# A written-out instruction order that counts one SBUF port for VectorE and GpSimd, with work moved between four engines

## The chip, the cores and the metric

The kernel runs on one core of a Trainium2 chip. The metric is the time of one execution in microseconds (us); the median of three runs of the kernel before is 695.69 us (695.14 to 697.32). Five engines work side by side, each through its own queue in order: TensorE (PE in the profile, its weight loads PEld), VectorE (DVE), ScalarE (ACT), GpSimd (POOL) and SyncE (SP, which only issues DMAs here). They meet through semaphores.

## The reference

Banded attention over 2 x 8 heads, 768 positions and 64 columns, then two MLPs on the 1536 tokens x 512 columns that come out:

```python
scores = q @ k.T / 8 - slope[h] * dist       # kept: the last 96 positions and the first 8
a = exp(scores - max); a = a / (sum(a) + 1e-9)
x = (a @ v) laid out as 1536 x 512
x = relu(x @ w_in) ** 2 @ w_out              # 512 -> 2048 -> 512
rms = sqrt(mean(x * x) + 1e-6); xn = x / rms * rms_g
g = xn @ w_gate                              # 512 -> 1536
out = (g * sigmoid(g) * (xn @ w_val)) @ w_out2
```

All inputs are float32 in value; the weights arrive as 64-bit numbers.

## The kernel before

Every large product is made of three matmuls (`mm3`, lines 310 to 323): an operand is split into a high part (a rounded copy, ScalarE, line 306) and a low part (the operand less the high part, line 307, on VectorE or GpSimd as the caller says), and high x high, high x low and low x high are added up in PSUM. A weight block arrives by DMA as 128 x 512 64-bit numbers; `expand` (lines 330 to 356) makes float32 of them with one ScalarE step (345) and four VectorE steps (346, 348, 350, 353), all in SBUF; then `split` makes its two parts. A helper `block` does this for one block, `pair` for two blocks at a time, of which it also forms sums and differences (line 388, GpSimd) for a seven-product scheme (`PRODUCTS`) that the second MLP uses.

Tokens are taken in four chunks of 384 columns. The attention works on 16 slices (4 chunks x 4 pairs of heads) of three tiles of 128 queries each. A slice's keys and queries are split in `prep`: high parts on GpSimd (lines 767 and 775; ScalarE only for the first), low parts on VectorE (769, 777). A tile (`tile`, from line 785) runs: six score matmuls (797); on VectorE a bias with a running minimum (804); on ScalarE the exponential with its sum (808); on GpSimd the addition of 1e-9 (812); on VectorE a reciprocal (815); on GpSimd the scaling of the two heads' probabilities (817); transposes on TensorE (824), an eviction (826) and the product with V (833).

The first MLP's products of chunks 0 to 2 for the first four blocks run beside the attention (`begin`), the rest behind it (`rest`): four groups of four blocks, each over four chunks, each chunk's `first` being 16 groups of three matmuls into a layer with relu and square (`relu2`, lines 413 to 416) and 16 more into the output, added up in y on VectorE (447). In the last group `norm_sum` follows each chunk: squares of y on ScalarE (464), their addition on VectorE (465), a matmul with ones into a PSUM bank (467), a square root (470) and three reciprocals (473). `norm` then forms, for a pair of chunks, the normalized x (494), differences (499, GpSimd) and the parts of all of them (306, 307). The second MLP takes six pairs of blocks, each over two pairs of chunks, through `quad` (lines 519 to 552; additions 535 and 543), the gated product (561, 565) and `final` (output bank added up in y, line 589).

The order of the instructions is written out by a planner (`Plan`, lines 60 to 156). Each operation has an engine, a duration from the formulas of lines 159 to 165, what it reads and writes, and for matmuls a due time, which is handed back to what they need. `solve` goes through planned time and starts, on the engine that is free first, the ready operation with the earliest due time. `emit` then issues all operations by planned start. On the chip the engines keep that order, each in its queue, and go when their semaphores allow. The planner holds the engines to be independent of one another. Ahead of the first real MLP product, spare matmuls (line 1096) fill planned idle time of TensorE.

Of the kernel before, what the change touches and what calls it, by code (L numbers as in the profile page):

```python
# [16 lines left out]
ALU = mybir.AluOpType  # L17
# [27 lines left out]
FILL = 30.0  # L45

# [9 lines left out]
class Op:  # L56
    __slots__ = ("slack", "eng", "dur", "lat", "emit", "deps", "succ", "due", "mode", "start", "end", "left", "ready", "n")


class Plan:  # L60
# [11 lines left out]
    def add(self, eng, dur, emit, r=(), w=(), due=None, mode=None, lat=None, slack=0.0):  # L72
# [4 lines left out]
        o.slack = slack  # L77
        o.deps, o.succ = set(), []
# [15 lines left out]
    def solve(self):  # L94
# [11 lines left out]
        self.fill, done, filling = [], 0, True  # L106
        while done < len(self.ops):
# [14 lines left out]
            o = heappop(ready[e])[2]  # L122
# [19 lines left out]
            free[e] = o.end  # L142
            done += 1
# [17 lines left out]
FAST = lambda n: 0.12 + n / 1920  # L161
ACT = lambda n: 0.10 + n / 1200
POOL1 = lambda n: 0.15 + n / 800
# [36 lines left out]
class Mlp:  # L200
# [101 lines left out]
    def split(self, src, dst, n, rs, ws, eng):  # L302
# [4 lines left out]
        self.op(eng, t(n), lambda: e.tensor_tensor(  # L307
            out=dst()[1], in0=src(), in1=f32(dst()[0]), op=ALU.subtract), rs + [(x, "hi") for x in ws], [(x, "lo") for x in ws])

    def mm3(self, bank, w, a, first, last, width, rs, due=None):  # L310
# [12 lines left out]
        return self.op("PE", dur, go, rs, [("b", bank)], due=due, mode="full")  # L323

# [5 lines left out]
    def expand(self):  # L330
# [16 lines left out]
            out=tl(bits), in0=tl(bits), scalar1=LEAST, scalar2=MOST, op0=ALU.max, op1=ALU.min), rb, rb)  # L347
        self.plan.add("DVE", FAST(512), lambda: v.tensor_scalar(  # L348
            out=bi(), in0=bi(), scalar1=3, scalar2=0x3FFFFFF8, op0=ALU.logical_shift_left, op1=ALU.bitwise_and), rb, rb)
        self.plan.add("DVE", DVE(512), lambda: v.scalar_tensor_tensor(  # L350
            out=bi(), in0=tl(raw)[:, :, 0], scalar=29, in1=bi(), op0=ALU.logical_shift_right, op1=ALU.bitwise_or),
            rr + rb, rb)
        self.plan.add("DVE", DVE(512), lambda: v.scalar_tensor_tensor(  # L353
            out=bi(), in0=tl(raw)[:, :, 1], scalar=-(1 << 30), in1=bi(), op0=ALU.bitwise_and, op1=ALU.bitwise_or),
            rr + rb, rb)
# [12 lines left out]
    def pair(self, key, slots):  # L368
# [6 lines left out]
        def keep(names, slot, parts=2):  # L375
# [6 lines left out]
        self.split(a, sl.get, 512, ra, sl.res, "POOL")  # L382
# [5 lines left out]
        add = lambda o, x, y, op, r, w: self.op("POOL", POOL2(256), lambda: nc.gpsimd.tensor_tensor(  # L388
            out=o(), in0=x(), in1=y(), op=op), r, w)
# [4 lines left out]
        self.split(s, sl2.get, 512, rs, sl2.res, "POOL")  # L394
# [7 lines left out]
        self.split(b, sl4.get, 512, rb, sl4.res, "POOL")  # L402
# [5 lines left out]
    def relu2(self, src, rsrc, act):  # L408
# [8 lines left out]
            out=get()[1], in0=t(), in1=f32(get()[0]), op=ALU.subtract), rt + hi, lo)  # L417
# [35 lines left out]
    def norm_sum(self, c, bank):  # L453
# [3 lines left out]
        for e in range(KD):  # L457
# [7 lines left out]
            self.op("DVE", DVE(CH), lambda t=t: nc.vector.tensor_tensor(out=s(), in0=s(), in1=t(), op=ALU.add), rs + rt, rs)  # L465
# [3 lines left out]
            due=self.clock, mode="full", slack=1.0)  # L469
# [6 lines left out]
    def norm(self, p):  # L476
# [4 lines left out]
        for q in range(2):  # L481
# [10 lines left out]
            def fin(n):  # L492
# [3 lines left out]
                    op0=ALU.mult, op1=ALU.mult), self.yres(e, c) + [("ns", c % 2)], res[n])  # L496

            def diff(n, x, y):
                self.op("POOL", POOL2(CH), lambda: nc.gpsimd.tensor_tensor(
                    out=tmp[n](), in0=tmp[x](), in1=tmp[y](), op=ALU.subtract), res[x] + res[y], res[n])  # L500

            def part(n):
                get, r = where[n]
                self.split(tmp[n], get, CH, res[n], r, "DVE")
# [94 lines left out]
    def weights(self, kind, g):  # L599

        if kind == "in" or kind == "out":
            for f in range(G1):
# [10 lines left out]
                self.block((kind, g * G1 + f), slot, "POOL")  # L613
        elif kind == "out2":
            self.used.setdefault(g, [])
            for f in range(2):
                slot = self.ring.popleft()
                self.used[g].append(slot)
                self.block((kind, 2 * g + f), slot, "POOL")
# [11 lines left out]
    def rest(self, clock):  # L631
# [21 lines left out]
        for kind in ("val", "out2"):  # L653
            self.weights(kind, 0)
        self.norm(1)
# [45 lines left out]
class Attention:  # L701
# [53 lines left out]
    def prep(self, s):  # L755

        nc, tl, i = self.nc, self.tl, s % 2
        for n, part in enumerate(self.pieces(s)):
# [5 lines left out]
            if n == 1:  # L764
                hp = self.slices[s][1]
                inv = lambda: tl("inv")[:, hp : hp + 1]
                self.op("POOL", POOL1(w), lambda raw=raw, hi=hi: nc.gpsimd.tensor_scalar(
                    out=hi(), in0=raw(), scalar1=inv(), scalar2=1.0, op0=ALU.mult, op1=ALU.mult), rr + ["inv"], rh)
# [404 lines left out]
```

## Time and profile before

| | |
|---|---|
| median of three runs | 695.69 us |
| profiled execution, its span | 696.2 us, 694.3 us |
| PE busy, PEld busy | 655.4 us (94%), 589.1 us (85%) |
| DVE busy | 487.7 us (70%) |
| ACT busy | 375.0 us (54%) |
| POOL busy | 262.7 us (38%) |
| mean granted TensorE clock | 0.992 |
| HBM read, written | 48.76 MB, 3.15 MB |

Busy time is from the first to the last cycle of an instruction as the profiler has it. Matmuls overlap, so PE busy overstates what TensorE did. A VectorE instruction that has begun but stands for something counts as busy. The stages by time: attention to about 164 us (with the first MLP's first products from 29 us), the rest of the first MLP to 394 us, the second MLP from about 395 us to 689 us, with the norm's work from 336 to 428 us among both.

### The profile page before, as it was taken

What the parts mean: (1) busy time and instruction counts of PE and PEld (TensorE: products, weight loads), DVE (VectorE), ACT (ScalarE), POOL (GpSimd) and SP (SyncE); (2) the same over time, 40 slices, a digit from 0 to 9 for tenths busy, and PEclk for the clock granted to TensorE, in tenths of its full rate; (3) what the DMA queues carried; (4) which work ended last, traced back from release to release, by engine and by line L of the source; (5) the groups of instructions that cost most, each with busy time, mean ns of one, the idle gap of its engine ahead of it and who ended that gap; (6) DMA issues with size and microseconds to landing.
All of it is one profiled execution on the core that took longest, in us unless ns stands there. A gap on an engine that the chain in (4) does not pass through costs nothing.

```text
span 694.3 us, 10667 instructions
## 1 busy us (share of the span) xinstructions
PE 655.4 (94%) x3827; PEld 589.1 (85%) x3827; DVE 487.7 (70%) x978; ACT 375.0 (54%) x834; POOL 262.7 (38%) x338
## 2 busy tenths in 40 slices
PE   5989999998999999999999888999999999999996
PEld 4667777777998999999999776899898898997994
DVE  6988964553889755238769999785966867768434
ACT  3758777776655554345655776554353443443320
POOL 3887855653333020015205245435144423342000
PEclk9989999999999999999999999999999999999999
DMA  5454443110443303002200000231120311210023
GB/s 197 157 171 155 141 141 91 61 46 3 134 139 121 122 22 102 0 1 92 72 21 1 31 30 25 69 121 31 61 91 31 112 62 41 92 61 0 2 76 110
DMA packets 18159, 52.69 MB, mean 76 GB/s; under 512 B 2608, under 2 KB 3888, under 8 KB 18096
## 3 DMA queue, kind: packets, MB, share of 16 engines
q1 hardware_dynamic: 18096, 51.92, 23.2%
q8 instruction: 32, 0.52, 0.3%
q14 instruction: 31, 0.25, 0.1%
HBM read 48.76 MB, written 3.15 MB: 75 GB/s over the span
## 4 chain that ended last, share of the span: by engine, by line
PE 68%; DVE 22%; ACT 4%; issue 2%; POOL 2%; DMA 0%; DVEq 0%; ACTq 0%; POOLq 0%
PE b L316 20%; PE b L317 19%; PE b L318 19%; PE ps L797 4%; PE av L833 3%; PE tb L824 3%; DVE wbits L350 3%; DVE wbits L348 3%; DVE h L416 2%; DVE wbits L346 2%; DVE wbits L353 2%; DVE xl L307 1%; DVE ra L565 1%; DVE h L307 1%; DVE nq L494 1%
## 5 line engine op out<-in xcount | busy, mean ns | idle before, releaser
L307 POOL TENSOR_TENSOR M<-wbits,M 128x512 fp32r<-128x512 f32 x68 | 94.1, 1385 | 207.9 <-ACT M L306 142.4
L316 PE MATMUL b<-xh,M 128*128 128x384 f32 x336 | 117.3, 349 | 2.5 <-DVE ra L565 1.3
L317 PE MATMUL b<-xl,M 128*128 128x384 f32 x336 | 114.2, 340 | 1.1 <-DVE xl L307 1.1
L318 PE MATMUL b<-xh,M 128*128 128x384 f32 x336 | 113.8, 339 | 0.5 <-POOL M L307 0.5
L316 PEld LDWEIGHTS b<-xh,M 128*128 128x128 f32 x336 | 63.9, 190 | 6.8 <-DVE ra L565 1.6
L416 DVE TENSOR_TENSOR h<-ra,h 128x384 fp32r<-128x384 f32 x64 | 43.7, 688 | 36.0 <-ACT ra L415 36.0
L317 PEld LDWEIGHTS b<-xl,M 128*128 128x128 f32 x336 | 64.0, 190 | 3.7 <-DVE xl L307 2.3
L817 POOL TENSOR_SCALAR p<-p,rs 128x256 f32<-128x256 f32 (+1 forms) x96 | 57.4, 610 | 21.7 <-DVE rs L815 20.3
L318 PEld LDWEIGHTS b<-xh,M 128*128 128x128 f32 x336 | 64.0, 190 | 0.8 <-POOL M L307 0.8
L306 ACT CAST M<-wbits 128x512 fp32r<-128x512 f32 x68 | 41.9, 617 | 40.2 <-DVE wbits L353 15.5
L317 PE MATMUL b<-h,M 128*128 128x384 f32 x176 | 59.8, 340 | 3.3 <-DVE h L416 3.3
L316 PE MATMUL b<-h,M 128*128 128x384 f32 x176 | 61.7, 350 | 0.3 <-ACT h L414 0.3
L589 DVE TENSOR_TENSOR y<-b,y 128x512 f32<-128x512 f32 x60 | 40.9, 688 | 28.5 <-PE b L318 28.1
L808 ACT ACTIVATE p<-p,mn 128x256 f32<-128x256 f32 (+1 forms) x96 | 46.7, 487 | 24.4 <-DVE mn L804 20.2
L316 PE MATMUL b<-M,h 128*128 128x512 f32 x144 | 56.6, 393 | 3.1 <-DVE y L589 3.0
L345 ACT ACTIVATE wbits<-wraw 128x512 f32<-128x512 f32 x68 | 45.2, 666 | 26.1 <-DMA wraw<-in_w_gate_dram 10.9
L318 PE MATMUL b<-h,M 128*128 128x384 f32 x176 | 59.0, 335 | 0.0
L350 DVE SCALAR_TENSOR_TENSOR wbits<-wraw,wbits 128x512 int32<-128x512 int32 x68 | 57.7, 848 | 1.7
L318 PE MATMUL b<-M,h 128*128 128x512 f32 x144 | 56.8, 395 | 0.8 <-DVE h L307 0.8
L317 PE MATMUL b<-M,h 128*128 128x512 f32 x144 | 56.6, 393 | 0.0
L353 DVE SCALAR_TENSOR_TENSOR wbits<-wraw,wbits 128x512 int32<-128x512 int32 x68 | 53.5, 791 | 1.1
L413 ACT ACTIVATE ra<-b 128x384 f32<-128x384 f32 x64 | 31.1, 486 | 38.9 <-PE b L318 37.7
(124 smaller groups left out, 1604.6 us busy)
## 6 DMA issues: line engine op xcount, KB each, us to landing
wraw<-in_w_out_dram SPq DMA_DIRECT2D x28, 512.0 KB, 3.4
wraw<-in_w_in_dram SPq DMA_DIRECT2D x16, 512.0 KB, 3.4
wraw<-in_w_gate_dram SPq DMA_DIRECT2D x12, 512.0 KB, 3.4
wraw<-in_w_val_dram SPq DMA_DIRECT2D x12, 512.0 KB, 3.4
raw<-in_kq_dram SPq DMA_DIRECT2D x8, 480.0 KB, 3.5
v<-in_vab_dram SPq DMA_DIRECT2D x8, 384.0 KB, 3.1
out_dram<-y SPq DMA_DIRECT2D x12, 256.0 KB, 2.3
raw<-in_kq_dram SPq DMA_DIRECT2D x7, 416.0 KB, 3.5
```

What stands on the lines that cost most here:

```text
L306: self.op("ACT", ACT(n), lambda: nc.scalar.copy(dst()[0], src()), rs, [(x, "hi") for x in ws])
L307: self.op(eng, t(n), lambda: e.tensor_tensor(out=dst()[1], in0=src(), in1=f32(dst()[0]), op=ALU.subtract), rs + [(x, "hi") for x in ws], [ ...
L316: nc.tensor.matmul(ps, lhsT=wh, rhs=ah, start=first, stop=False, skip_group_check=True)
L317: nc.tensor.matmul(ps, lhsT=wh, rhs=al, start=False, stop=False, skip_group_check=True)
L318: nc.tensor.matmul(ps, lhsT=wl, rhs=ah, start=False, stop=last, skip_group_check=True)
L345: self.plan.add("ACT", ACT(512), lambda: nc.scalar.activation(tl(bits), f32(tl(raw)[:, :, 1]), AF.Abs), rr, rb)
L350: self.plan.add("DVE", DVE(512), lambda: v.scalar_tensor_tensor(out=bi(), in0=tl(raw)[:, :, 0], scalar=29, in1=bi(), op0=ALU.logical_shift ...
L353: self.plan.add("DVE", DVE(512), lambda: v.scalar_tensor_tensor(out=bi(), in0=tl(raw)[:, :, 1], scalar=-(1 << 30), in1=bi(), op0=ALU.bitwi ...
L416: self.op("DVE", DVE(CH), lambda: nc.vector.tensor_tensor(out=get()[1], in0=t(), in1=f32(get()[0]), op=ALU.subtract), rt + hi, lo)
L589: self.op("DVE", DVE(DM), lambda tok=tok, ps=ps: nc.vector.tensor_tensor(out=self.o(tok), in0=ps(), in1=self.o(tok), op=ALU.add), [("b", b ...
L808: self.op("ACT", 0.33 + w / 1200, lambda j=j: nc.scalar.activation(tl(f"p{m}")[:, j, :w], tl(f"p{m}")[:, j, :w], AF.Exp, bias=tl(f"mn{m}") ...
L817: self.op("POOL", 0.2 + w / 800, lambda j=j: nc.gpsimd.tensor_scalar(out=tl(f"p{m}")[:, j, :w], in0=tl(f"p{m}")[:, j, :w], scalar1=rs()[:, ...
```

## The change

The planner gets a second resource: an operation can be marked as a user of the port that VectorE and GpSimd share. All GpSimd operations are, and VectorE's that read two SBUF operands or are marked so; operations with a PSUM operand are not. A port user starts no earlier than the end of the last port user on either engine; while the port is held, an engine takes a ready operation that doesn't use it, if it has one. Planned durations of four kinds are lowered (`FAST`, `ACT`, `POOL1`, and the costs of 804, 808, 815).

Engines change for four kinds of work: the scaling of probabilities goes from GpSimd to VectorE, the high parts of queries and keys from GpSimd to ScalarE, the low parts of the first eight weight blocks (`LO0`) and the differences of the norm from GpSimd to VectorE. What stays on GpSimd: the addition of 1e-9, all other low parts of weights, and the sums of line 388.

The matmul of the squares' sum of a chunk moves behind the next chunk's `first` and goes to bank 7 (before: bank 0 or 1, behind its own chunk), with a due time 12 us ahead of the planned clock there; the last chunk's stays at its end, in bank 1, behind the first weights of the second MLP. The first pair's norm thus follows chunk 2 and not chunk 1 in the program. The slack before such a matmul falls from 1.0 to 0.5 us.

```diff
+LO0, LO1, LOG, LOS = "DVE", "POOL", "POOL", "POOL"
+DIFF = ("DVE", "DVE")
+PART = ("DVE", "DVE")
+SUMS = "POOL"
+SCALE = ("DVE", "DVE")
+QHI = KHI = "ACT"
+EPS = "POOL"
+NSLACK = 0.5
...
+        o.port = eng == "POOL" if port is None else port
...
-            o = heappop(ready[e])[2]
+            if held > t + 0.05 and any(not x[2].port for x in ready[e]):
+                o = min(x for x in ready[e] if not x[2].port)[2]
+                ready[e].remove((o.due, o.n, o))
+                ready[e].sort()
+            else:
+                o = heappop(ready[e])[2]
+            if o.port:
+                t = max(t, held)
...
+            if o.port:
+                held = o.end
...
-FAST = lambda n: 0.12 + n / 1920
-ACT = lambda n: 0.10 + n / 1200
-POOL1 = lambda n: 0.15 + n / 800
+FAST = lambda n: 0.07 + n / 1920
+ACT = lambda n: 0.07 + n / 1200
+POOL1 = lambda n: 0.08 + n / 960
...
-            due=self.clock, mode="full", slack=1.0)
+            due=self.clock - (12.0 if bank == 7 else 0.0), mode="full", slack=NSLACK)
...
-                self.op("POOL", POOL2(CH), lambda: nc.gpsimd.tensor_tensor(
-                    out=tmp[n](), in0=tmp[x](), in1=tmp[y](), op=ALU.subtract), res[x] + res[y], res[n])
+                self.op(DIFF[p], POOL2(CH) if DIFF[p] == "POOL" else DVE(CH), lambda: self.eng(DIFF[p]).tensor_tensor(
+                    out=tmp[n](), in0=tmp[x](), in1=tmp[y](), op=ALU.subtract), res[x] + res[y], res[n], port=True)
...
-                self.block((kind, g * G1 + f), slot, "POOL")
+                self.block((kind, g * G1 + f), slot, LO0 if g == 0 else LO1)
...
-                if g == N1 - 1:
-                    self.norm_sum(c, c % 2)
-                    if c == 1:
+                if g == N1 - 1 and c:
+                    self.norm_sum(c - 1, 7)
+                    if c == 2:
                         self.norm(0)
...
+        self.norm_sum(NC_ - 1, 1)
         self.norm(1)
...
+                if QHI == "ACT":
+                    self.op("ACT", ACT(w), lambda raw=raw, hi=hi, inv=inv: nc.scalar.activation(
+                        hi(), raw(), AF.Copy, scale=inv()), rr + ["inv"], rh)
...
-            if s == 0:
+            if s == 0 or KHI == "ACT":
                 self.op("ACT", ACT(w), lambda raw=raw, hi=hi: nc.scalar.copy(hi(), raw()), rr, rh)
...
-            self.op("POOL", 0.2 + w / 800, lambda j=j: nc.gpsimd.tensor_scalar(
+            e = SCALE[j]
+            self.op(e, 0.12 + w / 760 if e == "POOL" else FAST(w), lambda j=j, e=e: self.mlp.eng(e).tensor_scalar(
                 out=tl(f"p{m}")[:, j, :w], in0=tl(f"p{m}")[:, j, :w], scalar1=rs()[:, j : j + 1], scalar2=1.0,
-                op0=ALU.mult, op1=ALU.mult), [("rs", m), ("p", m, j)], [("p", m, j)])
+                op0=ALU.mult, op1=ALU.mult), [("rs", m), ("p", m, j)], [("p", m, j)], port=True)
```

## Rows read from the trace of the kernel before

**Rows 1.** Stretches, columns: length, busy us (instructions) of each engine, clock, DMA.

```profile
280.00:300.00 20.00, 20.00 (x117) 20.00 (x116) 6.06 (x11) 6.18 (x12) 0.00 (x0) 1.00 0.00 1
499.00:546.50 47.50, 46.31 (x241) 42.62 (x240) 35.22 (x63) 20.28 (x41) 17.28 (x16) 1.00 0.20 67
```

**Rows 2.** Stretches, the five stages: PE, PEld, DVE, ACT, POOL busy, clock, DMA.

```profile
20.00:80.00 60.00, 54.95 (x412) 40.86 (x409) 52.42 (x144) 43.98 (x127) 50.53 (x76) 0.94 0.51 162
80.00:160.00 80.00, 80.00 (x639) 63.16 (x638) 45.38 (x171) 59.67 (x175) 45.53 (x94) 1.00 0.29 87
160.00:380.00 220.00, 213.51 (x1228) 208.88 (x1228) 146.97 (x232) 122.40 (x236) 54.96 (x46) 1.00 0.21 65
380.00:440.00 60.00, 51.88 (x255) 45.21 (x254) 54.70 (x82) 40.02 (x81) 28.89 (x25) 0.97 0.11 36
440.00:680.00 240.00, 234.49 (x1218) 215.92 (x1217) 168.96 (x292) 100.82 (x198) 73.54 (x68) 1.00 0.18 60
```

**Rows 3.** Waits of TensorE, whole span: us in total, times, longest.

```profile
PE b L317 <- DVE h L416: 5.6, 11, 1.2
...
PE b L316 <- DVE y L589: 3.0, 4, 0.8
```

**Rows 4.** Timeline, 43 to 46 us: start, us, what, idle time before it.

```profile
43.46 1.26 POOL L307 TENSOR_TENSOR M<-wbits,M 128x512 fp32r<-128x512 f32 x1
43.52 1.61 DVE L769 SCALAR_TENSOR_TENSOR kql<-raw,inv,kqh 128x384 fp32r<-128x384 f32 x1 [0.40 <-POOL kqh L767]
...
45.71 0.69 PE L833 MATMUL av<-pt,v 128*64 128x128 f32 x4 [2.14 <-issue]
```

**Rows 5.** Single lines: durations in ns, min/median/max, first and last start.

```profile
L348 DVE TENSOR_SCALAR wbits<-wbits x68: 410/427/1521, 14.0 to 633.3; 128x512 int32<-128x512 int32 x68
L350 DVE SCALAR_TENSOR_TENSOR wbits<-wraw,wbits x68: 680/693/1773, 16.3 to 635.1; 128x512 int32<-128x512 int32 x68
L769 DVE SCALAR_TENSOR_TENSOR kql<-raw,inv,kqh x16: 597/827/1644, 8.0 to 140.6; 128x384 fp32r<-128x384 f32 x16
L817 POOL TENSOR_SCALAR p<-p,rs x96: 368/480/1293, 13.7 to 160.4; 128x256 f32<-128x256 f32 x80, 128x128 f32<-128x128 f32 x16
```

**Rows 6.** Stretches of 5 us, columns as in rows 2.

```profile
45.00:50.00 5.00, 4.29 (x19) 3.33 (x20) 3.99 (x16) 1.98 (x6) 2.92 (x7) 0.53 0.57 172
```

**Rows 7.** Timeline, 539 to 544 us.

```profile
539.99 1.29 POOL L307 TENSOR_TENSOR M<-wbits,M 128x512 fp32r<-128x512 f32 x1 [6.07 <-ACT M L306]
540.11 1.72 DVE L350 SCALAR_TENSOR_TENSOR wbits<-wraw,wbits 128x512 int32<-128x512 int32 x1
...
543.21 0.51 PE L316 MATMUL b<-M,h 128*128 128x512 f32 x1 [0.75 <-DVE y L589]
```

**Rows 8.** Groups by line and form: busy us, mean ns, idle before.

```profile
L499 POOL TENSOR_TENSOR nq<-nq,nq 128x384 f32<-128x384 f32 x16 | 20.2, 1264 | 45.7 <-DVE nq L494 40.2 <-ACT h L306 2.6 <-ACT y L586 2.5
L465 DVE TENSOR_TENSOR ns<-ns,nq 128x384 f32<-128x384 f32 x12 | 8.0, 669 | 0.8 <-ACT nq L464 0.2
L773 ACT CAST kqh<-raw 128x448 fp32r<-128x448 f32 x1 | 0.6, 564 | 2.9 <-DMA raw<-in_kq_dram 2.9
L864 DVE TENSOR_SCALAR rel<-y 128x256 f32<-128x256 f32 x1 | 0.3, 286 | 0.0
```

**Rows 9.** Stretch 20 to 80 us, of lines 348, 353, 769 and 817 alone.

```profile
20.00:80.00 60.00, 5.22 (x8) 0.94 0.51 162
20.00:80.00 60.00, 7.68 (x8) 0.94 0.51 162
20.00:80.00 60.00, 7.13 (x6) 0.94 0.51 162
20.00:80.00 60.00, 24.67 (x38) 0.94 0.51 162
```

**Rows 10.** Timeline about 339 us; line 467 alone, durations as in rows 5.

```profile
338.77 1.02 DVE L447 TENSOR_TENSOR y<-b,y 128x384 f32<-128x384 f32 x2
...
L467 PE MATMUL b<-ns,ones x8: 483/486/590, 342.6 to 399.2; 128*128 128x384 f32 x8
```

More of the change, by code (lines that the diff above doesn't have):

```diff
@@ L56 @@
 class Op:
-    __slots__ = ("slack", "eng", "dur", "lat", "emit", "deps", "succ", "due", "mode", "start", "end", "left", "ready", "n")
+    __slots__ = ("slack", "port", "eng", "dur", "lat", "emit", "deps", "succ", "due", "mode", "start", "end", "left", "ready", "n")
 class Plan:
@@ L70, in __init__, with add @@
         self.last_fill = None
-    def add(self, eng, dur, emit, r=(), w=(), due=None, mode=None, lat=None, slack=0.0):
+    def add(self, eng, dur, emit, r=(), w=(), due=None, mode=None, lat=None, slack=0.0, port=None):
         o = Op()
@@ L105, in solve @@
                 heappush(wait[o.eng], (0.0, o.n, o))
-        self.fill, done, filling = [], 0, True
+        self.fill, done, filling, held = [], 0, True, 0.0
         while done < len(self.ops):
@@ L307, in split @@
         self.op(eng, t(n), lambda: e.tensor_tensor(
-            out=dst()[1], in0=src(), in1=f32(dst()[0]), op=ALU.subtract), rs + [(x, "hi") for x in ws], [(x, "lo") for x in ws])
+            out=dst()[1], in0=src(), in1=f32(dst()[0]), op=ALU.subtract), rs + [(x, "hi") for x in ws], [(x, "lo") for x in ws], port=not psum)
     def mm3(self, bank, w, a, first, last, width, rs, due=None):
@@ L323, in mm3, with eng @@
         return self.op("PE", dur, go, rs, [("b", bank)], due=due, mode="full")
+    def eng(self, name):
+        return self.nc.vector if name == "DVE" else self.nc.gpsimd
     def both(self, res):
@@ L381, in pair @@
         sl = slots()
-        self.split(a, sl.get, 512, ra, sl.res, "POOL")
+        self.split(a, sl.get, 512, ra, sl.res, LOG)
         keep(("A11", "A12"), sl)
@@ L387, in pair @@
         s, rs = (lambda: tl(f"wbits{n}")), [("bits", n)]
-        add = lambda o, x, y, op, r, w: self.op("POOL", POOL2(256), lambda: nc.gpsimd.tensor_tensor(
-            out=o(), in0=x(), in1=y(), op=op), r, w)
+        add = lambda o, x, y, op, r, w: self.op(
+            SUMS, POOL2(256) if SUMS == "POOL" else DVE(256), lambda: self.eng(SUMS).tensor_tensor(
+                out=o(), in0=x(), in1=y(), op=op), r, w, port=True)
         R = lambda x, i: (lambda: row(x)[:, i])
@@ L393, in pair @@
         sl2 = slots()
-        self.split(s, sl2.get, 512, rs, sl2.res, "POOL")
+        self.split(s, sl2.get, 512, rs, sl2.res, LOS)
         keep(("S1", "S2"), sl2)
@@ L401, in pair @@
         sl4 = slots()
-        self.split(b, sl4.get, 512, rb, sl4.res, "POOL")
+        self.split(b, sl4.get, 512, rb, sl4.res, LOS)
         keep(("S3", "S4"), sl4)
@@ L416, in relu2 @@
         self.op("DVE", DVE(CH), lambda: nc.vector.tensor_tensor(
-            out=get()[1], in0=t(), in1=f32(get()[0]), op=ALU.subtract), rt + hi, lo)
+            out=get()[1], in0=t(), in1=f32(get()[0]), op=ALU.subtract), rt + hi, lo, port=True)
     def first(self, g, c, banks, dues=None, k_major=False):
@@ L464, in norm_sum @@
             self.op("ACT", ACT(CH), lambda e=e, t=t: nc.scalar.activation(t(), self.y(e, c), AF.Square), self.yres(e, c), rt)
-            self.op("DVE", DVE(CH), lambda t=t: nc.vector.tensor_tensor(out=s(), in0=s(), in1=t(), op=ALU.add), rs + rt, rs)
+            self.op("DVE", DVE(CH), lambda t=t: nc.vector.tensor_tensor(out=s(), in0=s(), in1=t(), op=ALU.add), rs + rt, rs, port=True)
         ps = lambda: tl(f"b{bank}")[:, :CH]
@@ L618, in weights @@
                 self.used[g].append(slot)
-                self.block((kind, 2 * g + f), slot, "POOL")
+                self.block((kind, 2 * g + f), slot, LOG)
         else:
@@ L777, in prep @@
             self.op("DVE", DVE(w), lambda raw=raw, hi=hi, lo=lo: nc.vector.tensor_tensor(
-                out=lo(), in0=raw(), in1=f32(hi()), op=ALU.subtract), rr + rh, rl)
+                out=lo(), in0=raw(), in1=f32(hi()), op=ALU.subtract), rr + rh, rl, port=True)
     def at(self, n):
@@ L803, in tile @@
             name = "rel" if i else "t0"
-            self.op("DVE", DVE(w) + 0.09, lambda j=j, name=name: nc.vector.tensor_tensor_reduce(
+            self.op("DVE", DVE(w) + 0.01, lambda j=j, name=name: nc.vector.tensor_tensor_reduce(
                 out=tl(f"p{m}")[:, j, :w], in0=tl(f"ps{j}")[:, :w], in1=tl(name)[:, :w], scale=-0.125 * slope8(2 * hp + j), scalar=3.0e38,
@@ L839, in tile @@
             x = lambda: self.mlp.x(hp, c * CH, c * CH + CH)
-            self.mlp.split(lambda: tl("av"), x, CH, [("av", a) for a in range(NT)], self.mlp.xres(hp, c * CH, c * CH + CH), "DVE")
+            self.mlp.split(lambda: tl("av"), x, CH, [("av", a) for a in range(NT)], self.mlp.xres(hp, c * CH, c * CH + CH), "DVE", True)
     def masks(self):
```

27 lines of the change are left out of this document (14 added, 13 removed).

## The prediction

> **What bounds the kernel now.** I read the busy table of the page first, then the stages, then the waits of TensorE, then single stretches of the timeline. TensorE is called busy for 94% of the span, but a busy matmul overlaps its neighbour, so I count matmuls instead. In 280 to 300 us nothing disturbs TensorE: 117 matmuls in 20 us, 0.171 us each [rows 1]. Against that pace each stage shows what it loses [rows 2]:
>
> - 20 to 80 us (attention with the first MLP chunk beside it): 412 matmuls in 60 us, while 80 to 160 us, the same mix, runs 639 in 80 us (0.125 us each). 67 are missing, 8.4 us.
> - 80 to 160 us: TensorE is busy throughout; I count no loss.
> - 160 to 380 us (first MLP): 1228 matmuls x 0.171 = 210 of 220 us; 10 us lost, some of it the last attention tile.
> - 380 to 440 us (norm, and the step to the second MLP): 255 matmuls, 43.6 us at 0.171, about 46 us since the wide ones of the output take longer: 14 us lost.
> - 440 to 680 us (second MLP): one pair of blocks takes 47.5 us and has 240 matmuls [rows 1], 168 of 384 columns and 72 of 512. At 0.171 and 0.228 (0.171 x 512/384, an estimate) that is 45.1 us: 2.4 us lost in each of five, 12 us.
>
> So some 44 us of 696 are TensorE's to win; the head of the span and the tail behind the last matmul stay. The Trainium skill ("Trainium Kernel Development and Optimization", Performance Expectations) calls matmul busy time a bad measure and weight-load busy time a good one. By matmul busy, 440 to 680 us loses 5.5 us, by weight loads 24 us; my count lies between them, and the sum does not use either.
>
> Why TensorE waits: VectorE is late. The waits name line 416 (5.6 us) and line 589 (3.0 us), both VectorE [rows 3]. And VectorE is late where GpSimd runs: at 43.46 us GpSimd starts a lo part of 1.26 us; VectorE's line 769, begun 0.06 us later, takes 1.61 us instead of its 0.60 as if it had begun when GpSimd ended; TensorE then stands 2.14 us [rows 4, 5], and behind that its granted clock is 0.53 in 45 to 50 us [rows 6], nearly all at the lower level (1.2 of 2.4 GHz). Over the whole stage the clock is 0.94, so 0.06 x 60 = 3.6 us of full-speed work are gone; over 380 to 440 us it is 0.97, 1.8 us [rows 2]. In the second MLP a lo part on GpSimd at 539.99 us turns line 350's 0.69 us into 1.72 us, and TensorE waits 0.75 us at 543.21 us for the addition queued behind it [rows 5, 7].
>
> The Trainium skill ("SBUF — State Buffer", SBUF: two separate sides) says that VectorE (two SBUF inputs, or a two-port mode) and GpSimd share a port pair as an exclusive lock for whole instructions. The trace agrees: 1.01 us too long beside a 1.26 us operation.
>
> **The change part by part.**
>
> *The plan treats port users as one resource.* It issues no instruction. It can only order: while a GpSimd operation holds the port, VectorE is given work that reads PSUM. What it is worth is the VectorE lateness that it hides, bounded below by a loss (an order that is worse for TensorE) and above by the losses counted above. In 440 to 680 us no engine assignment of the weights changes, so this part acts alone there; a pair shows a wait of 0.75 us [rows 7], and the pipe runs empty and refills around it, which I put at as much again. I take 1 of the 2.4 us in each of five: **-5 us** (+3 to -10).
>
> *Scaling of probabilities, POOL to VectorE.* 96 instructions leave POOL (480 ns median [rows 5]). On VectorE the nearest row is line 864's 128x256 tensor_scalar, 0.286 us [rows 8]; by half of line 348's 0.427 us for 512 it would be 0.21 us [rows 5], by POOL's own price 0.48 us. I take 0.286, which has the same shape and engine. A GpSimd-to-TensorE hop becomes a VectorE-to-TensorE hop, and two scales shorten by 2 x 0.19 us in a tile's chain.
>
> *Lo parts of the first eight blocks, POOL to VectorE.* 8 x 0.69 us (line 350's clean price, same 512 width and SBUF inputs [rows 5]) = 5.5 us more VectorE.
>
> *High parts of K and Q, POOL to ScalarE.* 31 casts at up to 0.564 us [rows 8], some 17 us on ScalarE over the attention. In 80 to 160 us about half of them fall, 9 us on 59.7 busy of 80 [rows 2]: covered. Without that cover they would cost their 17 us; I cost them nothing.
>
> *What the opening comes to.* VectorE is busy 52.4 of 60 us in 20 to 80 us [rows 2]. Lines 348, 353 and 769 hold 5.22 - 8 x 0.427 = 1.8, 7.68 - 8 x 0.69 = 2.2 (353 by line 350's clean price, the same shape) and 7.13 - 6 x 0.60 = 3.5 us of waiting behind GpSimd [rows 5, 9], 7.5 us, which goes when GpSimd has little left there but the small addition of 1e-9. Added: 38 scales [rows 9] x 0.286 = 10.9, and 5.5. Result 52.4 - 7.5 + 16.4 = 61.3 of 60; with the low price of the scale 58, with POOL's price and no contention gone 76. So the opening stays bound by VectorE, with some of its weight work put off: the 2.14 us stall and the 3.6 us of slow clock can go, but VectorE has no room to give all of it. I take **-2 us** (+8 to -8).
>
> *160 to 380 us.* Lo parts of the later blocks and the sums stay on POOL; only the order is new. Of line 416's waits, 5.6 us in all [rows 3], I put most of it here, since the line runs 64 times and only the first chunks fall into the attention; I read its lateness as line 350's. I take **-4 us** (+2 to -8).
>
> *The norm.* 16 differences go from POOL (1.264 us) to VectorE; the nearest VectorE row is line 465, 0.669 us with waiting in it [rows 8]. 380 to 440 us has nine of them: VectorE gains about 9 x 0.55 = 5 us of work (0.55 is 0.669 less its waiting, an estimate) and is busy 54.7 of 60 already [rows 2], but it loses the waiting behind 11 us of GpSimd. The difference sits between two VectorE steps, so 0.6 to 0.7 us and two hops go from each link of a chain. The sum's matmul moves to bank 7 and behind the next chunk's first layer: for chunks 0 to 2 that is at least 8 us later than the chunk's end (16 groups of 3 x 0.171), where it now comes about 3 us after (chunk 0's last addition ends at 339.8 us, its sum's matmul starts at 342.6 us [rows 10]); the first norm has a whole chunk more to spare, so I cost it nothing; if it hadn't, the price is the 5 us between. What is late next is the second norm, from the last chunk, whose sum keeps bank 1. It stays a VectorE chain. I take **-5 us**, 1.8 of it clock (+4 to -10).
>
> *Slack 0.5 for 1.0 and the new prices:* a planned matmul comes up to 0.5 us earlier, four times: between -2 and +2 us, nothing taken.
>
> Sum: 2 + 4 + 5 + 5 = 16 us. The profiled execution took 696.2 us (span 694.3 and 1.9 around it), so 680.2; the median of the three runs is 0.5 us below the profiled one: **680 us**.
>
> **The rivals.**
>
> 1. *The forecast* (680, own range 672 to 688): half of the second MLP's and a third of the other losses go. For it: the stretched operations stand directly ahead of TensorE's waits. Against: VectorE's load in two stages.
> 2. *The order fills the opening and the norm too.* With chains shortened and the slow-clock stretches gone, 20 to 80 us gives 6 us more, the norm 4, the first MLP 5: 665 us. For it: all four losses have VectorE waiting behind GpSimd. Against: 61.3 of 60 us.
> 3. *The plan's port does not meet the chip's.* Engines run on semaphores, not on planned times; a GpSimd operation half a microsecond off collides with another VectorE operation instead, and the waits move. Then only work leaving POOL counts, and VectorE pays it back: 690 to 700, around 695.
> 4. *VectorE becomes the bound of the opening: slower.* Place: 20 to 80 us and the norm. Price: if scales cost 0.35 us (a quarter over the row, between it and POOL's 0.48) and contention stays, VectorE needs 52.4 + 13.3 + 5.5 = 71.2 us, 11.2 over; with 5 us won back in the two MLPs, 696.2 + 11.2 - 5 = 702 us. It decides once VectorE's work there passes 60 us by more than can be put off to 80 to 160 us, where it is busy 45 of 80: a block's expansion is 2 x 0.43 + 2 x 0.69 = 2.2 us [rows 5], two blocks can wait, so from about 64 us. The lock that the Trainium skill names ("SBUF — State Buffer", the same section) speaks against the change: a two-port scale also shuts out POOL's addition of 1e-9, which stays in the tile's chain; no row here shows that pair. Had each of 48 tiles to wait a scale's 0.286 us, 14 us would come, mostly beside other tiles, and the time would be that of this rival.
>
> **How the numbers follow.** Chances: forecast 0.48, rival 2 0.22, rival 3 0.14, rival 4 0.16. What can be told from no change is 0.3%, 2.1 us. Faster: 0.48 + 0.22 + 0.06 of rival 3 = 0.76; within: 0.07 (rival 3, and a little of 4); slower: 0.17. Range: a tenth lies below 663 (beyond rival 2) and a tenth above 698 (most of rival 4), so 663 to 698.
>
> **What would show it.** Right: lines 348, 350 and 353 with means near 0.43 and 0.69 us; no clock below 0.9 between 40 and 60 us; line 589's waits under 1.5 us; the pair of blocks at 46.5 us instead of 47.5; line 416's waits halved. Wrong: VectorE at 57 or more of 60 us with fewer than 412 matmuls in 20 to 80 us (rival 4), attention's last tile after 162 us, a norm whose matmul of squares is waited for, or the waits of line 416 and 589 as long as now under other names (rival 3).

## The result and the profile after

The changed kernel takes 677.57 us (median of four runs, 676.58 to 680.09) against 695.54 us of the kernel before beside it: a ratio of 0.9742, 95% interval 0.9711 to 0.9774. The profiled execution is the slowest of the four, 680.09 us with a span of 678.3 us, 16.1 us less than the profiled one of before.

The same five stretches as in [rows 2], of the changed kernel:

```profile
20.00:80.00 60.00, 56.89 (x408) 42.58 (x407) 55.40 (x185) 50.17 (x135) 5.42 (x17) 0.89 0.50 157
80.00:160.00 80.00, 79.56 (x625) 61.52 (x626) 58.38 (x226) 64.29 (x188) 6.06 (x27) 1.00 0.28 91
160.00:380.00 220.00, 217.64 (x1254) 215.60 (x1251) 148.29 (x250) 128.97 (x251) 47.88 (x38) 0.99 0.20 65
380.00:440.00 60.00, 54.60 (x271) 49.61 (x270) 52.98 (x92) 37.87 (x73) 17.86 (x16) 0.91 0.11 36
440.00:680.00 240.00, 231.52 (x1204) 214.04 (x1202) 167.19 (x291) 94.82 (x191) 71.53 (x66) 0.99 0.20 67
```

GpSimd is almost gone from the attention (50.5 to 5.4 us in the first stretch), but TensorE has no more matmuls there (408 for 412). The first MLP has 26 more in the same 220 us; the last stretch ends behind the kernel's last matmul now, so its count can't be compared. Pairs of blocks of the second MLP can: each pair but the first makes twelve additions into y (line 611, 589 before). The 49th of them starts here, before and now:

```profile
663.63 0.69 DVE L589 TENSOR_TENSOR y<-b,y 128x512 f32<-128x512 f32 x1 [0.83 <-PE b L318]
```

```profile
647.47 0.69 DVE L611 TENSOR_TENSOR y<-b,y 128x512 f32<-128x512 f32 x1 [0.83 <-PE b L336]
```

The first starts at 474.2 and 464.2 us (further down), so four pairs take 189.4 us before and 183.3 us now, about 47.4 and 45.8 us each. In the stretch of one pair, 45.2 us long now, TensorE doesn't stop (in [rows 1] it was busy for 46.31 of 47.5):

```profile
484.60:529.80 45.20, 45.20 (x239) 42.22 (x238) 34.80 (x62) 19.34 (x40) 16.82 (x16) 1.00 0.22 70
```

TensorE's longest waits are in other places than in [rows 3]. Line 438 is line 416 of before, and line 611, the addition into y of the second MLP, is in no row. The longest is for a high part of the attention's first slice (2.9 us before); the next two rows lie at 401 to 408 us, in the second norm:

```profile
PE ps L824 <- ACT kqh L791: 3.2, 1, 3.2
PE b L334 <- ACT xh L324: 2.8, 2, 1.6
PE b L335 <- DVE xl L325: 2.0, 2, 1.2
...
PE b L335 <- DVE h L438: 0.7, 1, 0.7
```

Where the 16 us come from is read off three lines, by first and last start: the product with V (its last start ends the attention), the addition into y of the first MLP, and that of the second. Of the kernel before:

```profile
L833 PE MATMUL av<-pt,v x352: 272/273/473, 17.7 to 164.1; 128*64 128x128 f32 x176
L447 DVE TENSOR_TENSOR y<-b,y x48: 494/552/558, 197.3 to 394.3; 128x384 f32<-128x384 f32 x48
L589 DVE TENSOR_TENSOR y<-b,y x60: 681/691/693, 474.2 to 688.5; 128x512 f32<-128x512 f32 x60
```

Of the changed one:

```profile
L861 PE MATMUL av<-pt,v x352: 272/273/476, 15.2 to 163.3; 128*64 128x128 f32 x176
L469 DVE TENSOR_TENSOR y<-b,y x48: 494/551/558, 195.7 to 389.4; 128x384 f32<-128x384 f32 x48
L611 DVE TENSOR_TENSOR y<-b,y x60: 674/691/692, 464.2 to 672.3; 128x512 f32<-128x512 f32 x60
```

Attention 164.1 to 163.3 us (-0.8). First MLP, from there to its last addition, 230.2 to 226.1 (-4.1). The norm with the first pair of blocks, to the second MLP's first addition, 79.9 to 74.8 (-5.1). The rest of the second MLP 214.3 to 208.1 (-6.2). The sum is 16.2 us.

The border between the first MLP and the norm is not the same place in the two orders. The two stages before and now (columns as in [rows 2]):

```profile
164.10:394.30 230.20, 223.13 (x1265) 217.89 (x1260) 160.22 (x253) 131.46 (x256) 57.86 (x47) 1.00 0.20 65
394.30:474.20 79.90, 73.14 (x370) 65.91 (x369) 68.94 (x108) 49.51 (x96) 37.17 (x33) 0.98 0.17 53
```

```profile
163.30:389.40 226.10, 224.47 (x1283) 222.99 (x1280) 157.35 (x264) 133.15 (x259) 49.99 (x40) 0.99 0.20 66
389.40:464.20 74.80, 69.40 (x349) 63.44 (x348) 61.36 (x107) 47.70 (x91) 26.18 (x24) 0.93 0.15 50
```

Now 18 matmuls more stand ahead of the border and 21 fewer behind it, 3 to 4 us at the 0.171 us of [rows 1] (an estimate). TensorE's idle time (length less busy) fell from 7.1 to 1.6 us in the first MLP and from 6.8 to 5.4 us in the norm. So only the sum of the two, 9.2 us, can be compared between kernels, and most of it was won in the first MLP.

TensorE's clock did not mend in this execution but fell earlier: it is at its lower level from 25 to 35 us and again in the norm.

```profile
25.00:30.00 5.00, 5.00 (x26) 3.35 (x27) 4.18 (x19) 3.48 (x12) 1.05 (x2) 0.50 0.50 166
30.00:35.00 5.00, 5.00 (x27) 3.21 (x23) 4.40 (x15) 3.78 (x11) 0.26 (x1) 0.50 0.44 157
...
405.00:410.00 5.00, 3.11 (x7) 2.21 (x8) 4.86 (x10) 2.29 (x5) 0.00 (x0) 0.50 0.00 0
```

### The profile page after: what moved, and what is told of

Its sections match the earlier page's. It is cut to its first block, busy times and chain, and to the rows that moved or that the text cites. A ratio compares the mean times of both kernels' runs of the same rounds, so it can differ in the third digit from the quotient of the medians.

```text
span 678.3 us, 10579 instructions
## 1 busy us (share of the span) xinstructions
PE 653.2 (96%) x3823; PEld 592.3 (87%) x3823; DVE 496.6 (73%) x1098; ACT 387.6 (57%) x865; POOL 152.2 (22%) x187
## 5 line engine op out<-in xcount | busy, mean ns | idle before, releaser
L325 POOL TENSOR_TENSOR M<-wbits,M 128x512 fp32r<-128x512 f32 x60 | 83.0, 1387 | 246.3 <-ACT M L324 194.6
L438 DVE TENSOR_TENSOR h<-ra,h 128x384 fp32r<-128x384 f32 x64 | 37.3, 586 | 49.0 <-ACT ra L437 49.0
L435 ACT ACTIVATE ra<-b 128x384 f32<-128x384 f32 x64 | 31.2, 487 | 47.5 <-PE b L336 47.2
L366 ACT ACTIVATE wbits<-wraw 128x512 f32<-128x512 f32 x68 | 45.2, 668 | 20.7 <-DMA wraw<-in_w_in_dram 8.0
L371 DVE SCALAR_TENSOR_TENSOR wbits<-wraw,wbits 128x512 int32<-128x512 int32 x68 | 55.1, 811 | 1.5
L374 DVE SCALAR_TENSOR_TENSOR wbits<-wraw,wbits 128x512 int32<-128x512 int32 x68 | 48.4, 714 | 0.9
L839 POOL TENSOR_SCALAR rs<-sm 128x2 f32<-128x2 f32 x48 | 12.7, 265 | 143.4 <-ACT p L835 143.4
```

Of the source, the lines that this page charges most:

```text
L325: self.op(eng, t(n), lambda: e.tensor_tensor(out=dst()[1], in0=src(), in1=f32(dst()[0]), op=ALU.subtract), rs + [(x, "hi") for x in ws], [ ...
L366: self.plan.add("ACT", ACT(512), lambda: nc.scalar.activation(tl(bits), f32(tl(raw)[:, :, 1]), AF.Abs), rr, rb)
L435: self.op("ACT", ACT(CH), lambda: nc.scalar.activation(t(), src(), AF.Relu), rsrc, rt)
L438: self.op("DVE", DVE(CH), lambda: nc.vector.tensor_tensor(out=get()[1], in0=t(), in1=f32(get()[0]), op=ALU.subtract), rt + hi, lo, port=True)
```

## The experiments

The table has what every run gave, the four stages worked out as above from each kernel's own three lines (times in us, one profile each), and the ratio to the kernel before on the same chip. The first MLP and the norm are to be read together, as said above.

| kernel | attention | first MLP | norm | second MLP | median | ratio, 95% interval |
|---|---|---|---|---|---|---|
| before | 164.1 | 230.2 | 79.9 | 214.3 | 695.5 | 1 |
| changed | 163.3 | 226.1 | 74.8 | 208.1 | 677.57 | 0.9742 (0.9711 to 0.9774) |
| after_again | 164.4 | 224.6 | 75.2 | 208.2 | 677.92 | 0.9734 (0.9718 to 0.9751) |
| fill45 (same instructions) | 161.3 | 226.1 | 75.2 | 208.1 | 678.39 | 0.9747 (0.9724 to 0.9770) |
| plan_only | 163.9 | 226.1 | 74.4 | 208.2 | 680.53 | 0.9780 (0.9747 to 0.9813) |
| no_port | 161.3 | 236.8 | 80.5 | 214.3 | 700.45 | 1.0066 (1.0041 to 1.0091) |
| no_port_old_prices | 163.5 | 232.7 | 79.0 | 214.3 | 696.27 | 1.0025 (0.9995 to 1.0055) |
| no_port_mean | 171.6 | 227.5 | 75.7 | 208.3 | 690.85 | 0.9936 (0.9914 to 0.9957) |
| scale_pool | 159.0 | 226.2 | 73.9 | 208.1 | 675.83 | 0.9709 (0.9692 to 0.9727) |
| low_dve | 160.5 | 225.6 | 75.3 | 207.8 | 677.02 | 0.9728 (0.9706 to 0.9750) |
| norm_old | 162.0 | 222.6 | 77.0 | 208.1 | 675.57 | 0.9712 (0.9687 to 0.9738) |
| old_prices | 158.9 | 225.6 | 76.0 | 208.1 | 676.46 | 0.9729 (0.9711 to 0.9747) |
| norm_warm | 160.5 | 226.1 | 74.7 | 207.2 | 676.09 | 0.9725 (0.9703 to 0.9746) |
| best | 156.9 | 226.2 | 74.7 | 207.1 | 674.89 | 0.9696 (0.9676 to 0.9716) |

**plan_only: the new order and prices, no work moved.**

```diff
-LO0, LO1, LOG, LOS = "DVE", "POOL", "POOL", "POOL"
-DIFF = ("DVE", "DVE")
-SCALE = ("DVE", "DVE")
-QHI = KHI = "ACT"
-NSLACK = 0.5
+LO0, LO1, LOG, LOS = "POOL", "POOL", "POOL", "POOL"
+DIFF = ("POOL", "POOL")
+SCALE = ("POOL", "POOL")
+QHI = KHI = "POOL"
+NSLACK = 1.0
...
-                if g == N1 - 1 and c:
-                    self.norm_sum(c - 1, 7)
-                    if c == 2:
+                if g == N1 - 1:
+                    self.norm_sum(c, c % 2)
+                    if c == 1:
...
-        self.norm_sum(NC_ - 1, 1)
```

> The new planner with the port and the new prices, but every engine as before (scales, high parts of K and Q, low parts of the first eight blocks, differences all on GpSimd) and the squares' sum in its old place. Theory A (the order around the port wins the two MLPs; the moved work wins the norm): first MLP 4 us and second MLP 5 to 6 us shorter as in the changed kernel, pair of blocks near 45.3 us, opening and norm as before or a little better, 683 to 687 us. Rival B (the win is the work that left GpSimd, the plan's port doesn't meet the chip's): MLPs as before with the waits of line 589's kind still there, 692 to 697 us. Rival C (the opening suffers when a busy GpSimd is serialized in the plan): MLPs shorter but attention ends 5 us or more later, 688 to 692 us.

Its three lines:

```profile
L860 PE MATMUL av<-pt,v x352: 272/273/473, 17.4 to 163.9; 128*64 128x128 f32 x176
L469 DVE TENSOR_TENSOR y<-b,y x48: 496/557/559, 194.8 to 390.0; 128x384 f32<-128x384 f32 x48
L611 DVE TENSOR_TENSOR y<-b,y x60: 674/692/693, 464.4 to 672.6; 128x512 f32<-128x512 f32 x60
```

680.53 us: with every engine where it was, the new order wins some 15 of the 18 us, and more than theory A gave it, because the first MLP and the norm together (300.5 us) are as short as in the changed kernel (300.9, before 310.1). Rival B falls.

**no_port: the moved work, ordered without the port.**

```diff
-        o.port = eng == "POOL" if port is None else port
+        o.port = False
```

> The changed kernel with the port mark false for every operation, so the planner again holds VectorE and GpSimd independent; engines, prices and the place of the squares' sum stay as changed. Theory A: the second MLP goes back to 47 us or more per pair of blocks, line 611 (the addition into y) is waited for again, the first MLP gives back about 4 us, the norm keeps most of its gain, the opening is within 2 us of the changed kernel: 686 to 690 us. Rival B: everything stays, 676 to 680 us.

```profile
L861 PE MATMUL av<-pt,v x352: 272/273/476, 15.7 to 161.3; 128*64 128x128 f32 x176
L469 DVE TENSOR_TENSOR y<-b,y x48: 542/557/558, 194.6 to 398.1; 128x384 f32<-128x384 f32 x48
L611 DVE TENSOR_TENSOR y<-b,y x60: 683/691/692, 478.6 to 692.9; 128x512 f32<-128x512 f32 x60
```

700.45 us, worse than theory A's 686 to 690 and 0.7% slower than before. The waits are back under their new line numbers. From 160 to 400 us (first row) and from 440 us on (the two others):

```profile
PE b L335 <- DVE h L438: 8.6, 8, 2.3
```

```profile
PE b L334 <- DVE ra L565: 3.4, 6, 1.0
PE b L334 <- DVE y L611: 3.0, 4, 0.8
```

The second MLP is to the tenth that of before (214.3). The first MLP and the norm together take 317.3 us, 7.2 more than before, and 6.6 of them are in the first MLP, where of the moved work only the squares' sum and the first norm's differences fall. What else is different there are the prices, which the next kernel put back.

**no_port_old_prices.**

```diff
-        o.port = eng == "POOL" if port is None else port
+        o.port = False
...
-FAST = lambda n: 0.07 + n / 1920
-ACT = lambda n: 0.07 + n / 1200
-POOL1 = lambda n: 0.08 + n / 960
+FAST = lambda n: 0.12 + n / 1920
+ACT = lambda n: 0.10 + n / 1200
+POOL1 = lambda n: 0.15 + n / 800
```

The planned prices of lines 831, 835, 839 and 842 also went back.

> The changed kernel with the port mark false everywhere and the planned prices of before: only the moved work and the sum's new place remain of the change. Without the port but with the new prices the first MLP took 237 us where it took 230 before and 226 with the port. Theory H (lower prices make a plan without the port too hopeful, so VectorE is later than planned): first MLP back to 229 to 232 us, second MLP 215 us, 692 to 697 us. Rival I (moving the work costs the first MLP those 6 us by itself): first MLP 235 us or more, 698 to 703 us.

First MLP 232.7 us (H expected 229 to 232, I 235 or more): the lower prices cost the plan without a port some 4 of the 6.6 us. Most of the rest is the border:

```profile
163.50:396.20 232.70, 225.86 (x1277) 221.71 (x1274) 160.87 (x263) 133.41 (x258) 48.95 (x40) 0.99 0.19 64
```

12 matmuls more than before stand in it, some 2 us; with the norm it is 311.7 us for 310.1. 696.27 us, ratio 1.0025 with 1 in its interval: the moved work and the sum's new place alone give nothing.

**old_prices: the port, with the prices of before** (the lines of the last diff but for the first edit).

> The changed kernel with the planned prices of before (two-port VectorE steps 0.05 us dearer, ScalarE 0.03, GpSimd's one-input steps 0.07 to 0.1, the three softmax steps 0.04 to 0.08 us dearer). Theory F (the port in the plan does the work, the prices are trimming): both MLPs as in the changed kernel (226 and 209 us), attention within 2 us, 676 to 681 us. Rival G (the new prices are what lets the plan fit the chip): first MLP 230 us or more, 682 us or more.

676.46 us, and both MLPs as expected of theory F; the attention is over at 158.9 us, 2.4 us or more before that of any profile of the changed program (161.3 to 164.4, below). With the port no effect of the prices on the time is seen.

**no_port_mean: slack in place of the port.**

```diff
-        o.port = eng == "POOL" if port is None else port
+        o.port = False
...
-DVE = lambda n: 0.07 + n / 960
-FAST = lambda n: 0.07 + n / 1920
+DVE = lambda n: 0.22 + n / 960
+FAST = lambda n: 0.25 + n / 1920
```

> The changed kernel with the port mark false everywhere and VectorE's planned prices raised to about the mean durations that the trace of before shows with the waiting in them (512 wide: 0.75 us for two operands, 0.52 us for the two-port form, where the changed plan has 0.60 and 0.34). It asks whether the port is worth its knowing where VectorE stands, or only the slack that it puts into the plan. Theory J (place matters): second MLP 213 to 216 us and first MLP 228 us or more, as in the two kernels without the port, 690 to 698 us. Rival K (slack is enough): second MLP 209 to 210 us, first MLP 225 to 227 us, 676 to 683 us.

```profile
L861 PE MATMUL av<-pt,v x352: 272/273/477, 16.3 to 171.6; 128*64 128x128 f32 x176
L469 DVE TENSOR_TENSOR y<-b,y x48: 494/557/558, 202.5 to 399.1; 128x384 f32<-128x384 f32 x48
L611 DVE TENSOR_TENSOR y<-b,y x60: 678/692/692, 474.8 to 683.1; 128x512 f32<-128x512 f32 x60
```

Both theories were half wrong. In the second MLP (208.3) and nearly so in the first MLP and the norm (303.2 together), dearer VectorE prices do what the port does: rival K. In the attention they cost 7 to 11 us (171.6), so the total is 690.85, in J's range for another reason. What TensorE waits for there is ScalarE's eviction of line 854 (1.9 us in 3 waits in the changed kernel):

```profile
PE av L861 <- ACT pt L854: 9.8, 17, 1.8
```

Why the raised prices bring that about was not tested. They also fall on the score step of line 831, which reads PSUM.

Does the port spare VectorE collisions (instructions stretched beside one of GpSimd), or does it only place them better? Two expansion lines from 440 to 680 us, 26 instructions each; lines 348 and 350 of before:

```profile
440.00:680.00 240.00, 14.92 (x26) 1.00 0.18 60
440.00:680.00 240.00, 23.00 (x26) 1.00 0.18 60
```

and the same two of the changed kernel (369 and 371):

```profile
440.00:680.00 240.00, 11.69 (x26) 0.99 0.20 67
440.00:680.00 240.00, 19.13 (x26) 0.99 0.20 67
```

At their clean 0.427 and 0.693 us [rows 5] they would be 11.1 and 18.0. The two other expansion steps have what they had or a little more (11.58 and 19.73 before, 12.42 and 19.70 after), and the low part of h, in the same stretch, takes longer, 617 and 690 ns in the mean for 557: of the kernel before, of the changed one and of plan_only:

```profile
L307 DVE TENSOR_TENSOR h<-ra,h 128x384 fp32r<-128x384 f32 x43 | 24.0, 557 | 4.9 <-ACT h L306 4.8
```

```profile
L325 DVE TENSOR_TENSOR h<-ra,h 128x384 fp32r<-128x384 f32 x40 | 24.4, 617 | 4.7 <-ACT h L324 4.6
```

```profile
L325 DVE TENSOR_TENSOR h<-ra,h 128x384 fp32r<-128x384 f32 x40 | 27.5, 690 | 3.5 <-ACT h L324 3.4
```

In plan_only the four expansion steps (64.5 us for 69.2) and this line (27.5 for 24.0, with three instructions fewer) hold together about what they held before, and yet its second MLP is as short as the changed kernel's. TensorE's waits from 440 us on, of before, beside the 3.0 us for line 589 of [rows 3], and the only one left in the changed kernel and in plan_only:

```profile
PE b L316 <- DVE ra L543: 2.4, 5, 0.7
```

```profile
PE b L334 <- DVE ra L565: 0.7, 1, 0.7
```

Counted in the traces, 17 VectorE instructions of that stretch run over 0.15 us longer than their line's usual time before, 16 in the changed kernel, 24 in plan_only and 27 in no_port, all of them beside a GpSimd instruction. So the collisions have moved more than they have gone, to places where TensorE doesn't wait behind them.

**scale_pool: the scales back on GpSimd.**

```diff
-SCALE = ("DVE", "DVE")
+SCALE = ("POOL", "POOL")
```

> The changed kernel with the scaling of probabilities back on GpSimd, all else as changed. The attention ended 0.7 us earlier in the changed kernel than before. Theory A (VectorE bounds the opening, and the scale on it is about even: VectorE's own time up by 0.2 to 0.29 us each, waiting behind GpSimd's 0.48 us gone): within 3 us of the changed kernel, 676 to 681 us, attention's end moved by less than 3 us. Rival (the scale on VectorE is what holds the opening back): attention ends 5 us or more earlier, 671 to 673 us. Rival (GpSimd's scales would block VectorE): attention 5 us later, 682 to 685 us.

```profile
L861 PE MATMUL av<-pt,v x352: 272/273/324, 15.4 to 159.0; 128*64 128x128 f32 x176
L845 POOL TENSOR_SCALAR p<-p,rs 128x256 f32<-128x256 f32 x80 | 48.9, 623 | 34.9 <-DVE rs L842 29.0 <-PE tb L852 3.1 <-PE ps L824 2.2
```

675.83 us, within 3 us of the changed kernel as theory A had it. The attention ends 1.5 to 2.3 us before that of three kernels with the scales on VectorE and a full clock in the opening (160.5, 160.5, 161.3 in the table), but not before that of a fourth, old_prices (158.9). So the largest piece of moved work wins nothing; that it costs a microsecond or two is not shown. The intervals, 0.9692 to 0.9727 and 0.9718 to 0.9751 of after_again, overlap a little.

**low_dve: the low parts of the second MLP's weights on VectorE too.**

```diff
-LO0, LO1, LOG, LOS = "DVE", "POOL", "POOL", "POOL"
+LO0, LO1, LOG, LOS = "DVE", "POOL", "DVE", "DVE"
```

> The changed kernel with the low parts of the second MLP's weights (36 of 128x512) on VectorE as well; GpSimd keeps the sums of line 410 and the low parts of the first MLP's later blocks. VectorE is busy 167 of 240 us in the second MLP; added 36 x 0.69 = 25 us, gone some 8 us of waiting. Theory A: in the second MLP VectorE isn't the bound and the plan already hides GpSimd there, so nothing is won (pair of blocks 45 to 45.6 us), and the norm, which VectorE bounds, gets 2 to 4 us longer by the low parts that fall into it: 677 to 682 us. Rival (any GpSimd beside VectorE costs): 672 to 675 us.

677.02 us, second MLP 207.8: as theory A had it, but the 2 to 4 us that it gave the norm did not come (75.3). Less GpSimd wins nothing where the plan already hides it.

**norm_old: the squares' sum as before** (the lines of plan_only's diff for `norm_sum` and `NSLACK` alone).

> The changed kernel with the squares' sum back in bank 0 or 1 right behind its own chunk and the slack back at 1.0 us. Theory D (the kernel with only the planner changed had as short a norm as the changed one, so the place of the sum is worth nothing): within 2 us of the unedited changed kernel, 676 to 680 us. Rival E (the sum's new place wins part of the 5 us that the norm lost): the stretch from the last addition into y of the first MLP to the first of the second MLP, 74.3 us in the changed kernel, becomes 76 us or more and the time 679 to 683 us.

The norm is 77.0 us, which is E's sign, but the first MLP is 3.5 us shorter than in the changed kernel (222.6 for 226.1): together 299.6 against 300.9. No wait has moved; the border has:

```profile
162.00:384.60 222.60, 221.43 (x1268) 220.39 (x1264) 156.35 (x263) 131.81 (x257) 49.36 (x40) 0.99 0.20 67
```

That is 15 matmuls fewer ahead of it than in the changed kernel (1283). The sum's new place wins nothing: 675.57 us, theory D, if a little under its range.

**after_again and fill45: the opening's clock.** fill45's edit turned out to change nothing (no planned gap of TensorE is left behind 30 us), so its instructions on every engine are those of the changed kernel, and both are repeats.

```diff
-FILL = 30.0
+FILL = 45.0
```

> The changed kernel once more, unedited, to stand beside the three kernels of this set: 676 to 680 us. Its first profile has TensorE at half clock from 25 to 38 us and a mean clock of 0.979; a run that stays nearer 0.99 should end its attention 2 to 3 us earlier, near 161 us, with the rest of the stages as in the first profile.

> The changed kernel with the spare matmuls of the opening allowed up to planned time 45 us instead of 30; the first MLP product comes at 38 to 39 us. The changed kernel's granted clock in 20 to 40 us was 0.66 and 0.83 in two profiles. Theory L (the stretch without spare matmuls lets the clock fall, and what it costs the attention is 2 to 4 us): clock 0.97 or more in 20 to 40 us, attention over at 159 to 161 us, 674 to 676 us, with less spread. Rival M (VectorE bounds the opening, the clock is only a symptom, and spare matmuls stand in the way of the tiles'): attention at 161 to 164 us, 677 to 680 us.

One program, three profiles, in 20 to 40 us:

```profile
20.00:40.00 20.00, 19.02 (x113) 12.75 (x113) 16.75 (x66) 14.29 (x42) 2.20 (x7) 0.66 0.44 138
```

```profile
20.00:40.00 20.00, 17.61 (x124) 11.82 (x124) 18.46 (x71) 15.36 (x46) 2.30 (x7) 0.83 0.50 160
```

```profile
20.00:40.00 20.00, 18.67 (x151) 12.65 (x148) 18.82 (x71) 17.05 (x52) 2.88 (x8) 1.00 0.53 164
```

The clock was 0.66, 0.83 and 1.00, the attention's end 163.3, 164.4 and 161.3 us, the profiled times 680.09, 680.02 and 678.39. Theory L's remedy was not tried; what the profiles show is that a low clock there goes with 2 to 3 us, and that it varies from run to run. Which of the two causes the other is not shown.

**norm_warm: spare matmuls where TensorE waits for the second norm.**

```diff
+WARM = 36
...
+                if fp == 0 and p == 1:
+                    for _ in range(WARM):
+                        self.op("PE", 0.22, lambda: self.nc.tensor.matmul(
+                            self.tl("b7")[:, :P], lhsT=self.ones, rhs=self.ones, start=True, stop=True,
+                            skip_group_check=True), (), [("b", 7)], mode="full")
```

> The changed kernel with 36 spare matmuls of 128 columns (ones with ones, into bank 7) that the plan puts where TensorE waits for the second norm. The clock in 400 to 420 us was 0.74 in two profiles of the changed kernel, 5.2 us of full-speed work, of which some 10 us are waiting anyway. Theory L: the clock stays at 0.95 or more there, the first addition into y of the second MLP comes 1.5 to 3 us earlier after the last one of the first MLP (74.3 us now, 71.5 to 73 then), 675 to 676.5 us. Rival (the wait is VectorE's chain alone): clock high, stretch still 74 us, 677 to 679 us.

```profile
400.00:420.00 20.00, 19.74 (x117) 18.24 (x117) 18.04 (x35) 11.45 (x25) 3.57 (x3) 1.00 0.00 0
```

The clock is 1.00 there (0.74 in the changed kernel), and the stretch to the second MLP's first addition is 74.7 us as ever, the rival's sign: VectorE is busy for 18.04 of the 20 us, and with TensorE's clock up nothing came sooner. The rest of the second MLP was 0.9 us shorter, with five matmuls fewer in it, so the low clock took a microsecond at most. The median, 676.09 us, lies in theory L's range all the same.

**best.** `SCALE` as in scale_pool, `FILL` as in fill45 and the spare matmuls of norm_warm.

> The changed kernel with what looked good: scales back on GpSimd (675.8 us by itself), spare matmuls up to 45 us in the opening and 36 in the norm. If the three add up: attention over at 158 to 160 us, norm 71 to 73 us, 671 to 674 us. If the scale's gain was only the clock of the opening, which both remedies mend: 673 to 676 us.

674.89 us (672.65 to 675.40), a ratio of 0.9676 to 0.9716, just below after_again's 0.9718 to 0.9751: about 3 us better than the changed kernel, with the attention over at 156.9 us. The three gains do not add up to the 671 to 674 us; the norm stayed at 74.7 us. It is the best of the study, but not apart from scale_pool alone.

## Why the prediction was right, and where it wasn't

The time was right: 680 us forecast, 677.57 measured, and 16 us forecast against 16.1 in the profiled executions (18.0 in the medians, since the profiled one was the slowest of its four). That it came so close is in part luck: the second MLP gave 1.2 us more than its term and the opening 1.2 us less. By steps:

- *Second MLP, -5: right in place, a little small* (-6.2). The waits for line 589 and their refilling are gone. I took 1 of 2.4 us in each of five pairs; four pairs gave some 1.5 us each. The sign that I set for the collisions came only in part: the lines that were 348, 350 and 353 have means of 0.487, 0.811 and 0.714 us over the whole span (0.586, 0.848 and 0.791 before), not 0.43 and 0.69. VectorE still collides; TensorE no longer waits for it.
- *First MLP, -4, and norm, -5: right together* (-9.2 for -9), with line 416's waits from 5.6 to 0.7 us. Apart, -4.1 and -5.1 look right too, but that is the border: by the matmuls on either side of it the first MLP won some 7 us and the norm some 2 (an estimate).
- *The norm's cause was wrong.* I put its 5 us on the differences that left GpSimd and on the clock. plan_only, with the differences on GpSimd, has the same first MLP and norm; no_port_old_prices, with them on VectorE, has none of the gain (311.7 us for 310.1). It is the order, as in the MLPs. That the sum's place was worth nothing was right; that the first norm had the time to spare was too: from 380 to 440 us TensorE waits only at 401 to 409 us, for the second.
- *Opening, -2: -0.8 in the profile*, +0.3 and -2.8 in the two others of the same program. VectorE is nearly full, as forecast, but at 55.4 of 60 us instead of 61.3; that it bounds the stage is argued, not shown. More waiting behind GpSimd went than the three lines that I counted (lines 346 and 350 held 4.39 and 6.16 us for 8 instructions each, some 1.0 and 0.6 us over their medians), although a scale costs more than the price I took; the rest of the difference is open:

```profile
L845 DVE TENSOR_SCALAR p<-p,rs 128x256 f32<-128x256 f32 x80 | 24.7, 351 | 3.9 <-ACT pt L854 0.6
```

0.351 us for 0.286. Rival 4's lock on GpSimd's addition of 1e-9 did not come: line 839 has a mean of 265 ns, 272 before. Its sign, the attention's last tile after 162 us, could tell nothing: the kernel before ends at 164.1 us.
- *The clock* was, with the norm's cause, the step that failed. I expected 3.6 and 1.8 us of work back; in the profile the granted clock fell instead (0.89 and 0.91). My sign, no clock below 0.9 between 40 and 60 us, came all the same, because the fall had moved to 25 to 35 us. In the opening one profile of three had the full clock; norm_warm shows that in the norm it matters by a microsecond at most.
- *Rival 3* had the right price for a case that did not come about: with no port in the plan the moved work is worth nothing (696.27 us, where it said around 695). But the order alone is worth nearly everything (0.978). Its doubt about the port is still half right: collisions did move, and in the MLPs dearer prices without any port do as well. What counts there is that the plan lets VectorE be late. The port does it without spoiling the attention. *Rival 2*'s further 15 us did not come.

Open: whether the moved work is worth the 3 us between plan_only and the changed kernel (their intervals overlap), and what of it is; and why dearer prices spoil the attention.

## What to carry to other kernels

When an order is written out by a plan, a resource that the plan doesn't know shows as instructions far over their median in the trace, and as waits behind them on the engine that should never wait; put the resource into the plan before moving work. Its mean lateness alone did as well in the MLPs here and lost 7 to 11 us in the attention. Test order and placement apart: here the same moved work ran 0.7% slower or 2.6% faster according to the order it was given. A low clock beside a wait is a symptom until a kernel that keeps it up is faster.

## What the runs showed that I had not expected

Lowering planned prices towards the clean durations made the plan without the port worse (first MLP 232.7 to 236.8 us, one profile each; the intervals of the two ratios overlap), and left the plan with it as it was (225.6 and 226.1). And one program's mean granted clock ranged from 0.979 to 0.993 between runs of the changed kernel, with 680.09 us at the one end and 676.56 us at the other.
